# Turning the token rows of a mixture-of-experts stage by DMA instead of TensorE, and putting its last three slot tiles behind a runtime test

## The chip, the cores and the metric

The kernel runs on one core of one Trainium2 chip. The metric is the device time of one execution in microseconds. Three runs of the kernel before gave 461.12, 461.92 and 462.48 us, median 461.92 us. The profile shown below comes from one further execution of 458.04 us, whose span from first to last instruction is 456.3 us.

## The reference

The program is an attention block followed by a top-1 mixture of experts.

```python
q_n, k_n = rmsnorm(q, g_q), rmsnorm(k, g_k)
attn = softmax(q_n @ k_n.T / sqrt(64))          # 8 batches, 12 heads, 448 tokens, 64 wide
x = (attn @ v), heads side by side              # N = 3584 tokens, D = 768
y_dense = relu(x @ w1_dense) @ w2_dense         # hidden width F = 512
e = argmax(x @ w_gate);  g = softmax(x @ w_gate)[e]     # E = 8 experts
y_moe = g * (relu(x @ w1[e]) @ w2[e])
out = y_dense + y_moe
```

The inputs are one fixed draw. On it the eight experts receive 409, 528, 432, 430, 448, 366, 478 and 493 tokens.

## The kernel before

The first part (about 270 us of the span) computes the attention and, for each batch, the gate logits, the chosen expert and the dense hidden layer relu(x @ w1_dense). For each token it writes one record to a DRAM tensor `rec` of 704 words: the token's row x (768 bf16 values), its dense hidden row (512 bf16 values) and its gate weight. This part is the same before and after.

The second part works on *slot tiles*. The tokens of each expert are put into tiles of 128 slots, so that a tile belongs to one expert. The number of tiles depends on the data: it is the sum over the experts of the token count divided by 128, rounded up. The program is written out for the most that can occur, NTL = 28 + 8 - 1 = 35 tiles (`ntl`, `tsi` and `ts` in L536 to L545 count them at run time, and `tsi[E-1]` holds the total). Tiles past the total have no tokens: their scatter is dropped by an out-of-range index (`emp`, L590), but all their work is done.

For each tile t:

- `gather(t)` (L601): POOL issues an indirect DMA that brings 128 records into `xg`, 128 partitions x 704 words.
- `xtrans(t)` (L608): TensorE turns the 6 blocks of x (L612) and the 4 blocks of the dense hidden row (L617), each 128x128 bf16, into two PSUM tiles; VectorE copies them out as `xT` (L614) and `hdT` (L619).
- `gemm1(t)` (L621): TensorE loads the tile's expert number into a register and does 6 matmuls of 512 columns with that expert's w1 (L625); ScalarE applies ReLU and the gate weight, `hs` (L630).
- `htrans(t)` (L632): TensorE turns `hs` in 4 blocks (L635), ScalarE copies them out as `heT` (L637).
- `gemm2(t)` (L639): 8 matmuls with the dense w2 (L644) and 8 with the expert's w2 (L649), 384 columns each, all accumulated into one two-bank PSUM tile `yp`. VectorE copies one half out (L655), ScalarE the other (L656), and POOL issues an indirect DMA that scatters the rows to the output (L657).

The orders of PE and POOL are the order in which the code is written (`manual_schedule(engines={PE, POOL})`). The loop (L673) does for each t: gather(t+4), gemm1(t+1), xtrans(t+2), gemm2(t), htrans(t+1). So one tile's matmuls stand between the steps of its neighbour. The pool that holds the PSUM tile of L656 has one buffer (`psy`, bufs=1).

```python
for t in range(NTL):
    if t + 4 < NTL:
        gather(t + 4)
    if t == 0:
        nc.gpsimd.dma_start(*wjobs[-1])
    if t + 1 < NTL:
        gemm1(t + 1)
    if t + 2 < NTL:
        xtrans(t + 2)
    gemm2(t)
    if t + 1 < NTL:
        htrans(t + 1)
```

Of the kernel before, what the change touches and what calls it, by code (L numbers as in the profile page):

```python
# [9 lines left out]
F32 = mybir.dt.float32  # L10
BF16 = mybir.dt.bfloat16
I32 = mybir.dt.int32
# [6 lines left out]
def kernel(  # L19
# [25 lines left out]
    KD = Dm // P  # L45
    FT = F // P
    HD = Dm // 2
# [10 lines left out]
    ident = const.tile([P, P], BF16)  # L58
# [13 lines left out]
    NTL = N // P + E - 1  # L72
# [3 lines left out]
    GO = XH + F // 2  # L76
    RC = GO + 64
# [56 lines left out]
    with tc.tile_pool(name="a_ld", bufs=2) as ld, \  # L134
# [391 lines left out]
        run({PE, POOL, SP, DVE, ACT})  # L526

    with tc.tile_pool(name="m_sb", bufs=5) as sb, \
         tc.tile_pool(name="m_p1", bufs=3, space=bass.MemoryType.PSUM) as ps1, \
         tc.tile_pool(name="m_p2", bufs=2, space=bass.MemoryType.PSUM) as ps2, \  # L530
         tc.tile_pool(name="m_ph", bufs=1, space=bass.MemoryType.PSUM) as psh, \
         tc.tile_pool(name="m_py", bufs=1, space=bass.MemoryType.PSUM) as psy:

        cnt = counts[B % 2]
        cmp = one.tile([P, E, NM], F32, tag="w1")
# [20 lines left out]
        for c in (slice(0, NC4 // 2), slice(NC4 // 2, NC4)):  # L556
# [3 lines left out]
            for i in range(2):  # L560
                nc.vector.tensor_mul(val[:, i, :, c], tl[:, :, c],
                                     tok[:, i, c].unsqueeze(1).to_broadcast(shape))
        slp = ps2.tile([P, 2, NTL], F32, tag="he")
        for n in range(NC4):
            nc.tensor.matmul(slp, sel[:, n // 4, n % 4], val[:, :, :, n],
                             start=(n == 0), stop=(n == NC4 - 1))
# [10 lines left out]
                                ts[:1].unsqueeze(1).to_broadcast([1, NTL, E]), ALU.is_ge)  # L577
        te = one.tile([1, NTL], F32)
        nc.vector.tensor_reduce(te, tcm, AX.X, ALU.add)
        tei = one.tile([1, NTL], I32)  # L580
        nc.vector.tensor_scalar(tei, te, 1.0, None, op0=ALU.subtract)

# [13 lines left out]
        nc.vector.scalar_tensor_tensor(dest, in0=t2, scalar=float(S - J + 1), in1=emp,  # L596
                                       op0=ALU.subtract, op1=ALU.add)

        xgs, xTs, hdTs, hes, heTs, eregs, stores = {}, {}, {}, {}, {}, {}, []

        def gather(t):  # L601
            xg = sb.tile([P, RC], F32, tag="xg", name="xg")
            nc.gpsimd.indirect_dma_start(  # L603
                out=xg, out_offset=None, in_=rec,
                in_offset=bass.IndirectOffsetOnAxis(ap=row[:, t:t + 1], axis=0))
            xgs[t] = xg

        def xtrans(t):  # L608
            xb = xgs[t].bitcast(BF16)
            xp = ps1.tile([P, KD, P], BF16, tag="tr")  # L610
            for kk in range(KD):
                nc.tensor.transpose(xp[:, kk], xb[:, kk * P:(kk + 1) * P], ident)  # L612
            xTs[t] = sb.tile([P, KD, P], BF16, tag="xT", name="xT")
            nc.vector.tensor_copy(xTs[t], xp)  # L614
            hp = ps1.tile([P, FT, P], BF16, tag="tr")
            for i in range(FT):
                nc.tensor.transpose(hp[:, i], xb[:, Dm + i * P:Dm + (i + 1) * P], ident)  # L617
            hdTs[t] = sb.tile([P, FT, P], BF16, tag="hdT", name="hdT")
            nc.vector.tensor_copy(hdTs[t], hp)  # L619

        def gemm1(t):  # L621
            eregs[t] = nc.tensor.value_load(tei[:, t:t + 1], min_val=0, max_val=min(t, E - 1))
            he = ps2.tile([P, F], F32, tag="he")
            for kk in range(KD):
                nc.tensor.matmul(he, xTs[t][:, kk],  # L625
                                 we[:, bass.ds(eregs[t], 1), 0, kk * F:(kk + 1) * F]
                                 .rearrange("p o f -> p (o f)"),
                                 start=(kk == 0), stop=(kk == KD - 1))
            hes[t] = sb.tile([P, F], BF16, tag="hs", name="hs")
            nc.scalar.activation(hes[t], he, AF.Relu, scale=xgs[t][:, GO:GO + 1])  # L630

        def htrans(t):  # L632
            hp = psh.tile([P, FT, P], BF16, tag="hp")
            for i in range(FT):
                nc.tensor.transpose(hp[:, i], hes[t][:, i * P:(i + 1) * P], ident)  # L635
            heTs[t] = sb.tile([P, FT, P], BF16, tag="heT", name="heT")
            nc.scalar.copy(heTs[t], hp)  # L637

        def gemm2(t):  # L639

            yp = psy.tile([P, 2, 512], F32, tag="y")
            for i in range(FT):
                for dd in range(2):
                    nc.tensor.matmul(yp[:, dd, :HD], hdTs[t][:, i],  # L644
                                     wd2[:, i, dd * HD:(dd + 1) * HD],
                                     start=(i == 0), stop=False)
            for i in range(FT):
                for dd in range(2):
                    nc.tensor.matmul(yp[:, dd, :HD], heTs[t][:, i],  # L649
                                     we[:, bass.ds(eregs[t], 1), 1,  # L650
                                        i * Dm + dd * HD:i * Dm + (dd + 1) * HD]
                                     .rearrange("p o f -> p (o f)"),
                                     start=False, stop=(i == FT - 1))
            ys = sb.tile([P, 2, HD], F32, tag="ys")
            nc.vector.tensor_copy(ys[:, 0], yp[:, 0, :HD])  # L655
            nc.scalar.copy(ys[:, 1], yp[:, 1, :HD])  # L656
            i = nc.gpsimd.indirect_dma_start(  # L657
                out=out, out_offset=bass.IndirectOffsetOnAxis(ap=dest[:, t:t + 1], axis=0),
                in_=ys.rearrange("p a d -> p (a d)"), in_offset=None,
                bounds_check=N - 1, oob_is_err=False)  # L660

            for j in stores:
                tc.declare_no_dep(i.ins, j.ins, reason="each token has one slot")
            stores.append(i)

        with tc.manual_schedule(engines={PE, POOL}):
            for t in range(4):
                gather(t)
            for t in range(2):
                xtrans(t)  # L670
            gemm1(0)
            htrans(0)
            for t in range(NTL):  # L673
                if t + 4 < NTL:
                    gather(t + 4)
                if t == 0:
                    nc.gpsimd.dma_start(*wjobs[-1])
                if t + 1 < NTL:
                    gemm1(t + 1)
                if t + 2 < NTL:  # L680
                    xtrans(t + 2)
                gemm2(t)
                if t + 1 < NTL:
                    htrans(t + 1)


# [28 lines left out]
```

## Time and profile before

| what | value |
|---|---|
| median of 3 runs | 461.92 us |
| profiled execution, its own time | 458.04 us |
| its span | 456.3 us |
| TensorE busy over the span | 384.7 us (84%) |
| VectorE, ScalarE, GpSimd busy | 255.7, 238.8, 240.6 us |
| mean granted TensorE clock | 0.956 of full speed |
| slot tiles: from the first record's arrival to the end | 281.6 to 456.3 us |

The time of an execution is 1.7 us more than its span here, which lies outside the first and last instruction. "Busy" counts an engine's own instructions; TensorE's weight loads run beside its matmuls and are listed as PEld. Issue times of DMAs stand under the queue of the engine that issues them (SPq, POOLq), and the data moves later on 16 shared DMA engines.

### The profile page before, as it was taken

How to read it: one execution, taken by the hardware profiler on the slowest of the kernel's cores; microseconds unless marked ns; L12 is line 12 of the kernel's file. 1: busy time of each engine (PE TensorE's matmuls, PEld its weight loads, DVE VectorE, ACT ScalarE, POOL GpSimd, SP SyncE). 2: the span in 40 equal slices, each digit the busy share in tenths (PEclk: the TensorE clock that was granted, in tenths of full speed). 3: DMA queues.
4: the chain of work that ended last, by engine and by line, in shares of the span. 5: the costliest groups of instructions: out<-in, count | busy, mean ns of one | idle time of the engine just before them, and what ended most of it. 6: DMA issues, size and time to landing. Idle time of an engine off the chain costs nothing.

```text
span 456.3 us, 13950 instructions
## 1 busy us (share of the span) xinstructions
PE 384.7 (84%) x5628; PEld 239.3 (52%) x5628; DVE 255.7 (56%) x744; ACT 238.8 (52%) x394; POOL 240.6 (53%) x275
## 2 busy tenths in 40 slices
PE   0557777988969889798897954899999999999994
PEld 0234554555645556455564633466666666666662
DVE  2565679788897888978875553233232333323230
ACT  2735677785876868768687210333242333334241
POOL 2385887596775877759651105134444353444422
PEclk9999989998998999989999995999999999999998
DMA  8579395977979689796669984553544545354420
GB/s 212 185 112 244 100 249 144 225 153 222 228 229 213 135 241 225 230 213 139 157 100 200 178 194 133 110 172 121 174 129 147 165 137 167 127 171 154 161 95 1
DMA packets 49759, 76.32 MB, mean 167 GB/s; under 512 B 8541, under 2 KB 45661, under 8 KB 49696
## 3 DMA queue, kind: packets, MB, share of 16 engines
q0 software_dynamic: 24544, 43.31, 43.7%
q1 hardware_dynamic: 24832, 32.12, 22.4%
q8 instruction: 46, 0.75, 0.7%
q14 instruction: 17, 0.14, 0.1%
q10 hardware_dynamic: 320, 0.00, 0.0%
HBM read 73.98 MB, written 23.86 MB: 214 GB/s over the span
## 4 chain that ended last, share of the span: by engine, by line
issue 32%; DVE 21%; PE 21%; POOL 16%; ACT 4%; DMA 4%; POOLq 1%; ACTq 0%; DVEq 0%
DVE ssq L192 8%; PE ff L365 8%; POOL xg L603 7%; PE av L259 5%; DVE xa L268 4%; PE sc L241 3%; PE xt L278 3%; POOL out_dram L657 3%; POOL sq L187 3%; DVE y L227 2%; DVE y L229 2%; DMA records<-hd 2%; ACT we L244 2%; DVE y L211 2%; DMA gk<-in_g_k_dram 2%
## 5 line engine op out<-in xcount | busy, mean ns | idle before, releaser
L244 ACT ACTIVATE we<-sc 128x896 bf16<-128x896 f32 x168 | 147.0, 917 | 46.3 <-PE sc L241 45.7
L657 POOL DMA_INDIRECT out_dram<-ys,dest x35 | 35.3, 1010 | 95.2 <-ACT ys L656 90.5
L241 PE MATMUL sc<-y 64*64 64x448 bf16 x672 | 69.9, 408 | 7.9 <-ACT we L244 5.2
L637 ACT COPY heT<-hp 128x512 bf16<-128x512 bf16 x35 | 20.5, 585 | 91.7 <-PE hp L635 91.7
L259 PE MATMUL av<-va,we 64*128 64x65 bf16 x2688 | 63.9, 198 | 4.4 <-issue 3.5
L259 PEld LDWEIGHTS <-we 64*128 64x128 bf16 x2688 | 51.4, 99 | 26.4 <-issue 23.2
L211 POOL TENSOR_TENSOR y<-xk,r 128x448 bf16<-128x448 f32 x46 | 42.1, 937 | 41.7 <-ACT r L205 41.7
L192 DVE TENSOR_REDUCE ssq<-sq 128x7 f32<-128x448 f32 x96 | 55.4, 611 | 12.0 <-POOL sq L187 7.9
L655 DVE COPY ys<-yp 128x384 f32<-128x384 f32 x35 | 19.5, 558 | 72.5 <-issue 55.7
L365 PE MATMUL ff<-wd,xT 128*128 128x512 bf16 x192 | 52.1, 413 | 8.3 <-DVE xa L268 5.6
L625 PE MATMUL he<-we,xT 128*128 (+1 forms) x210 | 52.3, 386 | 0.5 <-issue 0.5
L644 PE MATMUL yp<-wd,hdT 128*128 128x384 bf16 x280 | 51.2, 326 | 1.1 <-ACT ys L656 1.1
L649 PE MATMUL yp<-we,heT 128*128 (+1 forms) x280 | 51.2, 326 | 0.0
L603 POOL DMA_INDIRECT xg<-records,row x35 | 34.5, 986 | 30.4 <-DVE t L591 20.0
L187 POOL TENSOR_TENSOR sq<-xk 128x448 f32<-128x448 f32 x44 | 40.7, 938 | 16.8 <-DVE ssq L192 16.7
L614 DVE COPY xT<-xp 128x768 bf16<-128x768 bf16 x35 | 19.5, 558 | 51.0 <-PE he L625 35.0
L219 PE MATMUL tr<-ident,y 128*128 128x128 bf16 x336 | 26.9, 237 | 20.0 <-DVE y L211 15.0
L268 DVE TENSOR_TENSOR xa<-av,inv 128x256 bf16<-128x256 f32 x96 | 40.8, 425 | 3.3
L187 POOL TENSOR_TENSOR sq<-xq 128x448 f32<-128x448 f32 x44 | 40.1, 932 | 0.0
L630 ACT ACTIVATE hs<-he,xg 128x512 bf16<-128x512 f32 x35 | 24.0, 687 | 27.8 <-PE he L625 18.1
L241 PEld LDWEIGHTS <-y 64*64 64x64 bf16 x672 | 20.5, 107 | 32.9 <-issue 22.9
L649 PEld LDWEIGHTS <-heT 128*128 128x128 bf16 x280 | 27.4, 98 | 18.1
(105 smaller groups left out, 475.6 us busy)
## 6 DMA issues: line engine op xcount, KB each, us to landing
we<-in_moe_w_dram POOLq DMA_DIRECT2D x16, 768.0 KB
xq<-in_q_dram SPq DMA_DIRECT2D x24, 448.0 KB, 4.8
xk<-in_k_dram SPq DMA_DIRECT2D x24, 448.0 KB, 5.7
xv<-in_v_dram POOLq DMA_DIRECT2D x11, 448.0 KB
records<-xa SPq DMA_DIRECT2D x8, 576.0 KB, 9.2
records<-hd SPq DMA_DIRECT2D x24, 128.0 KB, 3.9
wd<-in_moe_w_dense_dram POOLq DMA_DIRECT2D x2, 768.0 KB
records<-xa SPq DMA_DIRECT2D x8, 96.0 KB, 9.0
```

The lines of the kernel that those rows point to most:

```text
L187: nc.gpsimd.tensor_mul(sqs[name, g, hh], x, x)
L192: nc.vector.tensor_reduce(ssqs[g][:, "qk".index(name), hh], sqs[name, g, hh].rearrange("p (j d) -> p j d", d=D), AX.X, ALU.add)
L211: eng.tensor_mul(y[:, :, hh], xin[name, g][:, hh].rearrange("p (j d) -> p j d", d=D), rs[name, g][:, hh].unsqueeze(2).to_broadcast([P, J, D]))
L241: nc.tensor.matmul(ps[r * D:(r + 1) * D, hh, :S], kT[rows, r, j], qT[rows, r].rearrange("p j s -> p (j s)"), start=True, stop=True)
L244: nc.scalar.activation(x, ps[:, :, :S], AF.Exp, scale=scale)
L259: nc.tensor.matmul(avs[hh, r][:, m], exs[g, j][rows, hh, QC[m]:QC[m] + P], va[rows, hh, j, :De], start=(j == 0), stop=(j == J - 1))
L268: nc.vector.tensor_mul(xas[b][:, :, h * D:(h + 1) * D], avs[hh, r][:, :, :D], inv.to_broadcast([P, 4, D]))
L365: nc.tensor.matmul(ff[0], xTs[b][:, kk, QC[m]:QC[m] + P], wd1[:, kk], start=(kk == 0), stop=(kk == KD - 1))
L603: nc.gpsimd.indirect_dma_start(out=xg, out_offset=None, in_=rec, in_offset=bass.IndirectOffsetOnAxis(ap=row[:, t:t + 1], axis=0))
L625: nc.tensor.matmul(he, xTs[t][:, kk], we[:, bass.ds(eregs[t], 1), 0, kk * F:(kk + 1) * F] .rearrange("p o f -> p (o f)"), start=(kk == 0), ...
L644: nc.tensor.matmul(yp[:, dd, :HD], hdTs[t][:, i], wd2[:, i, dd * HD:(dd + 1) * HD], start=(i == 0), stop=False)
L649: nc.tensor.matmul(yp[:, dd, :HD], heTs[t][:, i], we[:, bass.ds(eregs[t], 1), 1, i * Dm + dd * HD:i * Dm + (dd + 1) * HD] .rearrange("p o ...
```

## The change

Only the second part changes.

- The rows of a tile are turned by one DMA transpose from `xg` to `xT`, issued on SP's queue, which carried nothing in this part before. `xT` now holds all 10 blocks, x and dense hidden row. The first two tiles are still turned by TensorE (`turn(t, True)`), now through one PSUM buffer `xp` for both groups of blocks.
- Gathers run five tiles ahead instead of four, with 7 buffers `xg` instead of 5. The transpose of tile t+5 is written right behind its gather.
- `yp` has two PSUM buffers instead of one. The copy of `heT` goes from ScalarE to VectorE.
- The first 32 tiles (NT1 = 28 + 4) are written out as before. All engines then load the run-time total of tiles, `tct`, and the last three tiles stand in a branch that is taken if the total is above 32.

```diff
-         tc.tile_pool(name="m_p1", bufs=3, space=bass.MemoryType.PSUM) as ps1, \
-         tc.tile_pool(name="m_p2", bufs=2, space=bass.MemoryType.PSUM) as ps2, \
-         tc.tile_pool(name="m_ph", bufs=1, space=bass.MemoryType.PSUM) as psh, \
-         tc.tile_pool(name="m_py", bufs=1, space=bass.MemoryType.PSUM) as psy:
+         tc.tile_pool(name="m_ph", bufs=2, space=bass.MemoryType.PSUM) as psh, \
+         tc.tile_pool(name="m_pt", bufs=1, space=bass.MemoryType.PSUM) as pst, \
+         tc.tile_pool(name="m_py", bufs=2, space=bass.MemoryType.PSUM) as psy:
...
+        tct = one.tile([1, 1], I32)
+        nc.vector.tensor_copy(tct, tsi[:1, E - 1:])
...
-            xg = sb.tile([P, RC], F32, tag="xg", name="xg")
+            xg = sb.tile([P, RC], F32, tag="xg", name="xg", bufs=7)
...
-        def xtrans(t):
+        def turn(t, here):
+
+            xTs[t] = sb.tile([P, KD + FT, P], BF16, tag="xT", name="xT")
             xb = xgs[t].bitcast(BF16)
-            xp = ps1.tile([P, KD, P], BF16, tag="tr")
-            for kk in range(KD):
-                nc.tensor.transpose(xp[:, kk], xb[:, kk * P:(kk + 1) * P], ident)
-            xTs[t] = sb.tile([P, KD, P], BF16, tag="xT", name="xT")
-            nc.vector.tensor_copy(xTs[t], xp)
-            hp = ps1.tile([P, FT, P], BF16, tag="tr")
-            for i in range(FT):
-                nc.tensor.transpose(hp[:, i], xb[:, Dm + i * P:Dm + (i + 1) * P], ident)
-            hdTs[t] = sb.tile([P, FT, P], BF16, tag="hdT", name="hdT")
-            nc.vector.tensor_copy(hdTs[t], hp)
+            if not here:
+                nc.sync.dma_start_transpose(xTs[t], xb[:, :2 * GO])
+                return
+            for c in (range(KD), range(KD, KD + FT)):
+                xp = pst.tile([P, KD, P], BF16, tag="xp", name="xp")
+                for i in c:
+                    nc.tensor.transpose(xp[:, i - c[0]], xb[:, i * P:(i + 1) * P], ident)
+                nc.vector.tensor_copy(xTs[t][:, c[0]:c[-1] + 1], xp[:, :len(c)])
...
-            nc.scalar.copy(heTs[t], hp)
+            nc.vector.tensor_copy(heTs[t], hp)
...
-                    nc.tensor.matmul(yp[:, dd, :HD], hdTs[t][:, i],
+                    nc.tensor.matmul(yp[:, dd, :HD], xTs[t][:, KD + i],
...
+        def slots(t0, t1, weights=None):
+            ahead = 5
+            for t in range(t0, min(t0 + ahead, t1)):
                 gather(t)
+            for t in range(t0 + 2, min(t0 + ahead, t1)):
+                turn(t, False)
+            turn(t0, True)
+            gemm1(t0)
+            turn(t0 + 1, True)
+            htrans(t0)
+            for t in range(t0, t1):
+                if t + ahead < t1:
+                    gather(t + ahead)
+                    turn(t + ahead, False)
+                if t == t0 and weights:
+                    nc.gpsimd.dma_start(*weights)
+                if t + 1 < t1:
+                    gemm1(t + 1)
                 gemm2(t)
+                if t + 1 < t1:
                     htrans(t + 1)
...
+        NT1 = N // P + E // 2
+        with tc.manual_schedule(engines={PE, POOL, SP}):
+            slots(0, NT1, wjobs[-1])
+        used = nc.values_load(tct, min_val=1, max_val=NTL)
+        with tc.If(used > NT1):
+            with tc.manual_schedule(engines={PE, POOL, SP}):
+                slots(NT1, NTL)
```

The order of TensorE in one turn of the loop, before, with what each step waits for (the eight rows are where one step ends and the next begins; `xT` and `hdT` are a tile's turned rows, `heT` its turned hidden layer):

```order
L625 LDWEIGHTS xT [waits DVE_49]
...
L612 LDWEIGHTS xg [waits DMASW0_49]
L612 MATMUL xp<-ident,xg 128x128
...
L617 LDWEIGHTS xg
L617 MATMUL hp<-ident,xg 128x128 [waits PE_49]
...
L644 LDWEIGHTS hdT
L644 MATMUL yp<-wd_92,hdT 128x384 [waits Activation_49]
...
L635 LDWEIGHTS hs [waits Activation_49]
```

The same turn after the change:

```order
L626 LDWEIGHTS xT [waits DMAHW3_49]
L626 ISA
L626 MATMUL he<-we,xT 128x512
...
L645 LDWEIGHTS xT
L645 MATMUL yp<-wd_92,xT 128x384
...
L650 LDWEIGHTS heT [waits DVE_49]
...
L636 LDWEIGHTS hs [waits Activation_49]
```

The transposes of L612 and L617 are gone from the turn, the first matmul step waits for a DMA of SP's queue instead of for VectorE, and the dense matmuls no longer wait for ScalarE.

SP's queue from the last store of the first part on, after the change (before, the second row was the last):

```order
L377 DMA records<-hd 128x256 [waits DMAHW2_49,Activation_49]
L377 DMA records<-hd 64x256 [waits DMAHW3_49,Activation_49]
L694 TENSOR_LOAD tct [waits DVE_49]
...
L614 DMA_TRANSPOSE xT<-xg 128x10x128 [waits DMASW3_49]
L614 DMA_TRANSPOSE xT<-xg 128x10x128 [waits DMASW4_49,DVE_49,PE_49]
...
L614 DMA_TRANSPOSE xT<-xg 128x10x128 [waits DMAHW4_49,DMASW1_49,PE_49]
...
L695 COMPARE_AND_BRANCH
```

There are 30 transposes ahead of the branch, one for each of the tiles 2 to 31. Each waits for its gather (a DMASW semaphore) and, through PE, for the matmuls that last read its `xT` buffer, those of the tile five before.

The end of POOL's order after the change:

```order
L658 DMA out_dram<-ys,dest 3584x768 [waits DMASW6_49,Activation_49]
L694 TENSOR_LOAD tct [waits DVE_49]
L695 COMPARE_AND_BRANCH
L604 DMA xg<-records,row 128x704 [waits DMAHW3_49,DMASW7_49]
...
L695 ISA [waits DMASW3_49,DMASW4_49,DMASW2_49,DMASW7_49,DMASW1_49,DMASW0_49]
L695 UNCONDITIONAL_BRANCH
L658 DMA out_dram<-ys,dest 3584x768 [waits DMASW7_49,Activation_49]
```

The first row is the scatter of tile 30, and the last row, which stands behind the branch, that of tile 31: POOL loads the total and branches between the two.

## Rows read from the trace of the kernel before

**Rows 1.** Busy time by stretch: length, engines (instructions), granted clock, DMA share, GB/s.

```profile
270.00:290.00 20.00, 10.84 (x71) 7.34 (x71) 3.91 (x14) 2.36 (x4) 5.78 (x6) 0.66 0.67 168
290.00:340.00 50.00, 50.00 (x391) 31.55 (x389) 15.36 (x32) 17.22 (x31) 20.02 (x20) 1.00 0.42 135
340.00:440.00 100.00, 100.00 (x775) 62.70 (x773) 30.95 (x64) 35.91 (x66) 40.96 (x41) 1.00 0.46 151
```

**Rows 2.** Timeline of one turn: start, length, engine, line, operation, what ended the idle time.

```profile
302.39 0.39 PE L635 MATMUL hp<-ident,hs 128*128 128x128 bf16 x4
...
302.62 1.46 PE L625 MATMUL he<-we,xT 128*128 x6
...
303.91 0.50 PE L612 MATMUL xp<-ident,xg 128*128 128x128 bf16 x6
304.06 1.02 POOL L657 DMA_INDIRECT out_dram<-ys,dest  x1 [2.36 <-ACT ys L656]
...
304.25 0.39 PE L617 MATMUL hp<-ident,xg 128*128 128x128 bf16 x4
...
304.47 1.46 PE L644 MATMUL yp<-wd,hdT 128*128 128x384 bf16 x8
...
305.38 0.99 POOL L603 DMA_INDIRECT xg<-records,row  x1 [0.31 <-issue]
```

**Rows 3.** Timeline: VectorE's copy of `ys` for tile 0, then the last tiles.

```profile
293.24 0.56 DVE L655 COPY ys<-yp 128x384 f32<-128x384 f32 x1 [1.93 <-PE yp L649]
...
442.95 0.56 DVE L655 COPY ys<-yp 128x384 f32<-128x384 f32 x1 [1.99 <-issue]
...
446.81 0.39 PE L635 MATMUL hp<-ident,hs 128*128 128x128 bf16 x4
447.07 0.56 DVE L655 COPY ys<-yp 128x384 f32<-128x384 f32 x1 [3.56 <-PE yp L649]
...
448.31 1.46 PE L644 MATMUL yp<-wd,hdT 128*128 128x384 bf16 x8 [1.11 <-ACT ys L656]
...
449.61 1.46 PE L649 MATMUL yp<-we,heT 128*128 x8
451.16 0.56 DVE L655 COPY ys<-yp 128x384 f32<-128x384 f32 x1 [3.54 <-PE yp L649]
451.75 0.48 ACT L656 COPY ys<-yp 128x384 f32<-128x384 f32 x1 [3.50 <-DVE ys L655]
452.50 0.98 POOL L657 DMA_INDIRECT out_dram<-ys,dest  x1 [2.99 <-ACT ys L656]
```

**Rows 4.** Groups of 290 to 457 us: count, busy us, mean ns of one, idle before.

```profile
L630 ACT ACTIVATE hs<-he,xg 128x512 bf16<-128x512 f32 x34 | 23.4, 687 | 12.2 <-ACT ys L656 9.8 <-PE he L625 2.4
L619 DVE COPY hdT<-hp 128x512 bf16<-128x512 bf16 x33 | 13.7, 415 | 0.0
```

**Rows 5.** DMA queues (packets, MB, share of 16 engines) and loads (KB each, us to landing).

```profile
q0 software_dynamic: 24544, 43.31, 43.7%
q1 hardware_dynamic: 24832, 32.12, 22.4%
q8 instruction: 46, 0.75, 0.7%
...
xk<-in_k_dram SPq DMA_DIRECT2D x24, 448.0 KB, 5.7
```

**Rows 6.** Timeline of the first tiles.

```profile
277.24 1.05 POOL L603 DMA_INDIRECT xg<-records,row  x1 [20.01 <-DVE t L591]
...
281.60 0.80 PE L612 MATMUL xp<-ident,xg 128*128 128x128 bf16 x6 [6.32 <-issue]
...
282.48 0.56 DVE L614 COPY xT<-xp 128x768 bf16<-128x768 bf16 x1 [4.90 <-DMA xg<-records,row]
...
283.55 0.63 PE L617 MATMUL hp<-ident,xg 128*128 128x128 bf16 x4
...
284.01 2.73 PE L625 MATMUL he<-we,xT 128*128 128x512 bf16 x6
...
288.59 1.46 PE L625 MATMUL he<-we,xT 128*128 x6 [0.54 <-issue]
```

More of the change, by code (lines that the diff above doesn't have):

```diff
@@ L562 @@
                                      tok[:, i, c].unsqueeze(1).to_broadcast(shape))
-        slp = ps2.tile([P, 2, NTL], F32, tag="he")
+        slp = psh.tile([P, 2, NTL], F32, tag="he")
         for n in range(NC4):
@@ L597 @@
                                        op0=ALU.subtract, op1=ALU.add)
-        xgs, xTs, hdTs, hes, heTs, eregs, stores = {}, {}, {}, {}, {}, {}, []
+        xgs, xTs, hes, heTs, eregs, stores = {}, {}, {}, {}, {}, []
         def gather(t):
-            xg = sb.tile([P, RC], F32, tag="xg", name="xg")
+            xg = sb.tile([P, RC], F32, tag="xg", name="xg", bufs=7)
             nc.gpsimd.indirect_dma_start(
@@ L606, in gather @@
             xgs[t] = xg
-        def xtrans(t):
+        def turn(t, here):
+            xTs[t] = sb.tile([P, KD + FT, P], BF16, tag="xT", name="xT")
             xb = xgs[t].bitcast(BF16)
-            xp = ps1.tile([P, KD, P], BF16, tag="tr")
-            for kk in range(KD):
-                nc.tensor.transpose(xp[:, kk], xb[:, kk * P:(kk + 1) * P], ident)
-            xTs[t] = sb.tile([P, KD, P], BF16, tag="xT", name="xT")
-            nc.vector.tensor_copy(xTs[t], xp)
-            hp = ps1.tile([P, FT, P], BF16, tag="tr")
-            for i in range(FT):
-                nc.tensor.transpose(hp[:, i], xb[:, Dm + i * P:Dm + (i + 1) * P], ident)
-            hdTs[t] = sb.tile([P, FT, P], BF16, tag="hdT", name="hdT")
-            nc.vector.tensor_copy(hdTs[t], hp)
+            if not here:
[6 more added lines that the diff above has]
+                nc.vector.tensor_copy(xTs[t][:, c[0]:c[-1] + 1], xp[:, :len(c)])
         def gemm1(t):
             eregs[t] = nc.tensor.value_load(tei[:, t:t + 1], min_val=0, max_val=min(t, E - 1))
-            he = ps2.tile([P, F], F32, tag="he")
+            he = psh.tile([P, F], F32, tag="he")
             for kk in range(KD):
@@ L632, in htrans @@
         def htrans(t):
-            hp = psh.tile([P, FT, P], BF16, tag="hp")
+            hp = pst.tile([P, FT, P], BF16, tag="hp")
             for i in range(FT):
@@ L664, in gemm2 @@
             stores.append(i)
-        with tc.manual_schedule(engines={PE, POOL}):
-            for t in range(4):
+        def slots(t0, t1, weights=None):
+            ahead = 5
+            for t in range(t0, min(t0 + ahead, t1)):
                 gather(t)
[L669 to L678, printed above, removed]
+            for t in range(t0 + 2, min(t0 + ahead, t1)):
[11 more added lines that the diff above has]
+                if t + 1 < t1:
                     gemm1(t + 1)
-                if t + 2 < NTL:
-                    xtrans(t + 2)
                 gemm2(t)
-                if t + 1 < NTL:
+                if t + 1 < t1:
                     htrans(t + 1)
+        NT1 = N // P + E // 2
[5 more added lines that the diff above has]
+                slots(NT1, NTL)
 _INS = ['q', 'k', 'v', 'g_q', 'g_k', 'moe_w_gate', 'moe_w1_dense', 'moe_w2_dense', 'moe_w1', 'moe_w2']
```

## The prediction

> **What bounds the kernel now.** I read the busy times by stretch first. From 290 us on TensorE is busy for the whole of every stretch, at the full one of its two clock levels, 2.4 GHz (granted 1.00), while VectorE and ScalarE work for under 40% of the time, POOL for some 40% and the DMA engines for 42% to 46% [rows 1]. So in the slot tiles each microsecond taken from TensorE's own stream is a microsecond of the end, until something else has less slack. The timeline of one turn gives that stream step by step [rows 2]. From the start of one step to the next: htrans 302.39 to 302.62 = 0.23 us, gemm1 302.62 to 303.91 = 1.29, the transposes of x 303.91 to 304.25 = 0.34 and of the hidden row 304.25 to 304.47 = 0.22; the rest are the two halves of gemm2. VectorE's copies of `ys` give the whole turn: from 293.24 (tile 0) to 442.95 (tile 32) are 32 turns, 4.68 us each [rows 3]. The two halves of gemm2 are thus 4.68 - 0.23 - 1.29 - 0.56 = 2.60 us, as the start of the second half, 449.61 - 448.31 = 1.30, confirms [rows 3].
>
> The trace even shows the turn without transposes: tile 33 is the first with none left to do, and its copy comes 447.07 - 442.95 = 4.12 us after the one before [rows 3], which is 4.68 - 0.56.
>
> **The change part by part.** All against the profiled execution: span 456.3 us, time 458.04 us, 3.9 us under the median of 461.92.
>
> *Transposes off TensorE.* The new turn is 4.12 us if the turned row is there in time. *Three tiles less.* The draw gives 4+5+4+4+4+3+4+4 = 32 tiles, so the branch is not taken and tile 31 is the last. Its last turn has no next gemm1: htrans and gemm2, 0.23 + 2.60 = 2.83 us. Before, the copies of tiles 0 and 34 were 451.16 - 293.24 = 157.92 us apart [rows 3]. After, tiles 0 and 31 are 30 x 4.12 + 2.83 = 126.4 us apart. **Gain 31.5 us**, some 17 of it from transposes and 14 from the tiles.
>
> *Second `yp` buffer, `heT` on VectorE.* Nothing on the path. The one wait for `yp` in the rows, 1.11 us for ScalarE's copy, came where a turn had neither gemm1 nor transposes [rows 3]; gemm1 alone (1.29 us) nearly covers it, and the second buffer removes it. VectorE gets a copy of 0.415 us for a tile (the row of the same shape, hdT) and loses 0.97 us; ScalarE keeps 0.687 for `hs` and 0.485 for `ys` [rows 3, 4]. Neither nears 4.12. If that cover were gone, the next to be late would be the copy of `heT`, which has gemm1 and half of gemm2 (2.6 us) to finish.
>
> *Start.* Tiles 0 and 1 stay on TensorE, now through one PSUM buffer: the second group of a tile waits for the copy of the first. Before, gemm1(0) began at 284.01, behind the transposes of both tiles [rows 6]. After: 281.60 + 0.80 + 0.56 (copy) + 0.63 plus two hand-overs of about 0.1 = 283.8; it runs to 286.5 at the low clock level (2.73 us for 6 matmuls that later take 1.29 to the next step) [rows 6]. Tile 1 then takes 0.82 (taken as tile 0's 0.80) + 0.56 + 0.63 + 0.41, so its gemm1 starts near 289.0 against 288.59 [rows 6], but no transposes of tile 2 (0.56) follow. I take 0; between -1 and +2.5, the latter if TensorE, with more gaps here, gets its full clock a few microseconds later (1.2 GHz, half speed).
>
> *Gathers and POOL.* Per turn still one gather (0.99) and one scatter (1.02) [rows 2]. Two more gathers before the loop's first scatter have been issued by 285, ahead of any scatter. Gather t+6 is behind scatter t, about 2.5 us after gemm2(t) ends; it lands some 4.3 us after its issue (277.24 to 281.60) [rows 6], so its transpose can start about 7 us after gemm2(t) and is wanted four turns, 16.5 us, after it. **The transpose has 9 us of latency to spare.** Its `xT` buffer is free earlier, after the first half of gemm2(t+1). Plain loads of 448 KB on SP's queue landed in 5.7 us beside a busier DMA [rows 5]. SP had nothing else to do in this part, so nothing is queued behind its waits but further transposes.
>
> *Transpose rate.* This is the unknown: the trace holds none. One moves 128 x 1,280 bf16 = 327,680 bytes. Today's DMA load per turn is 0.46 of 4.68 us = 2.15 us of all 16 engines for one gather and one scatter, 753,664 bytes [rows 1]. In a turn of 4.12 us it leaves 1.97 us. From below: a transpose priced as these bytes is 327,680/753,664 x 2.15 = 0.93 us, and the engines are 75% busy. From above: SP's shape is 128x10x128, so if each 256-byte row of a block is a packet of its own there are 1,280, and SP's queue has paid 0.224 x 456.3 x 16 / 24,832 = 0.066 us for a packet that was 1.3 KB on average [rows 5]: 1,280 x 0.066 / 16 = 5.3 us. I take under 1.97, because the nearest row is the SP loads, long rows between DRAM and SBUF at 32.12 MB in 22.4% of 16 engines x 456.3 us, 19.6 GB/s an engine, which makes 1.04 us. Then the rate is hidden and costs nothing.
>
> *Branch and end.* The last scatter now stands behind POOL's load of the total and its branch. POOL is free after scatter 30, about 1 us into a last turn of 2.83 us, so some 1.8 us are covered. A branch may have to bring its code: an instruction packet took 0.007 x 456.3 x 16 / 46 = 1.1 us [rows 5]. I take +1 us, between 0 and +4. The Trainium skill (Runtime: NRT & Kernel Launch, Instruction fetch mechanics) speaks against the branch: code is fetched sequentially, and a taken branch outside the two-page window waits for a DMA of the target page. No row here shows one; by that rule this term would stay positive on whichever engine ends last, and 0 would hold only if the target lies in the window.
>
> **Sum:** 458.04 - 31.5 + 0 + 1 = 427.5 us for a profile like this, 461.92 - 30.5 = 431.4, **about 432 us** as a median.
>
> **The rivals.** If transposes come every P us, their stream bounds the end instead: the first starts near 284, the thirtieth lands about 2 us after its slot, and gemm1(31), two gemm2 and htrans (6.7 us) follow it. The copy of tile 31 comes at 292.7 + 30 P, against 293.24 + 126.4 = 419.6 in the forecast. So P counts from 4.23 us on, 30 us for each microsecond, and the gain is used up at P = 4.23 + 30.5/30 = 5.25.
>
> *A. The DMA engines or SP pace the tiles a little.* P between 4.23 and 5.2, for instance a transpose of 2.5 us of all engines: 2.15 + 2.5 = 4.65, and 432 + 30 x 0.42 = 445 us. For it: the engines would be at 100%, and nothing shows a transpose is as cheap as a load. Against: needs twice the price of the nearest row.
>
> *B. Slower: transposes go through the DMA engines as 1,280 short packets.* It decides from P = 5.25, that is from a transpose of 3.1 us. At the upper bound 2.15 + 5.3 = 7.4 us: 432 + 30 x 3.2 = 528 us. TensorE then waits in each gemm1 for SP's DMA. For it: the shape, and that output partitions are written across input rows. Against: the mean price comes from long packets and should overstate short ones. The skill's page Advanced Engine Details and Errata (X-Bar Transpose) says that such DMAs are as fast as regular ones, which would leave 432; the same page (DGE: Hardware vs Software) lists transposes from a hardware queue, such as SP's, as the less efficient kind, without a figure. No run here has shown either.
>
> *C. It doesn't do what it says:* the count exceeds 32 and the branch runs. Three tiles more, 3 x 4.12 us, plus a new start of about 4.3 us (gather) and 7 us (281.60 to 288.59) [rows 6]: 432 + 24 = 456 us. Rounding in bf16 would have to move 16 tokens or more between experts (the nearest limit upwards is expert 5, 366 of 384).
>
> **How the numbers follow.** Forecast 0.66; A 0.15; B 0.17; C 0.02. A measurement of this kernel can tell about 0.3%, 1.4 us. The forecast and C are faster, and of A all but 0.03: faster 0.80, same 0.03, slower 0.17. The forecast's own range is 428 to 436 (start -1 to +2.5, end 0 to +4, partly together). To hold 8 in 10 the range goes on through most of A: 428 to 452; left out are B and the rest of A and C.
>
> **What would show it.** Right: `ys` copies of VectorE every 4.12 us, 32 of them; TensorE busy throughout from 290 us; SP's transposes landing within about 9 us and a DMA share near 0.75; the first matmul of gemm1 not waiting for DMA. A or B: idle time of TensorE in front of gemm1, ended by a DMA that writes `xT`, and copies further apart than 4.12. A wrong end term shows as idle POOL before the last scatter; a wrong start as a first `ys` copy away from 293.2. The prediction is wrong if the transposes' own spacing exceeds 4.23 us.

## The result and the profile after

The changed kernel took 445.43 us (median of 4 runs, 440.51 to 450.19), the kernel before 461.52 us in the same comparison (4 runs, 456.93 to 462.48): a ratio of 0.9635, 95% interval 0.9519 to 0.975. It is faster, as forecast, and inside the stated range of 428 to 452, but 13 us over the predicted 432. The profiled execution took 444.17 us, span 442.5. (Of all profiles below only that of the kernel with the two groups apart is of a disturbed execution, 456.9 us at a lower granted clock; no distance is taken from it.)

Four distances of the two traces tell where the 16.7 us over the predicted span of 425.8 went. The prediction rests on the rows of before in [rows 3, 6].

| distance, us | before | predicted | after |
|---|---|---|---|
| span start to the first gather | 277.24 | 277.24 | 278.86 |
| first gather to the `ys` copy of tile 0 | 16.00 | 16.00 | 16.27 |
| that copy to the copy of the last tile | 157.92 | 126.4 | 137.14 |
| that copy to the end of the span | 5.14 | 6.1 | 10.23 |

The first is the part that the change leaves alone: 1.6 us. Executions with the same code up to there also differ by that much and more (276.7 us with four leading tiles, 282.2 with the late load). The start was as forecast. Missing are 10.7 us in the tiles and 4.1 us at the end.

From the busy times by stretch (length, PE, PEld, DVE, ACT, POOL with counts, clock, DMA share, GB/s) of the kernel after:

```profile
290.00:300.00 10.00, 4.88 (x34) 2.88 (x32) 1.64 (x4) 1.17 (x2) 2.03 (x2) 0.99 1.36 101
300.00:310.00 10.00, 9.76 (x50) 5.17 (x51) 0.89 (x2) 1.85 (x3) 2.01 (x2) 0.83 1.24 144
360.00:380.00 20.00, 19.83 (x128) 11.53 (x126) 3.80 (x9) 5.35 (x9) 9.99 (x10) 1.00 1.10 253
```

Against [rows 1] TensorE lost half of the stretch from 290 us, and the DMA share, 0.46 before, is above 1 through the tiles. Such a share must count packets that are open side by side on one engine, so it is no share of the engines' work. The prediction had 0.75.

The timeline of the first tiles shows the loss:

```profile
278.86 1.05 POOL L604 DMA_INDIRECT xg<-records,row  x1 [18.14 <-DVE t L592]
...
285.99 14.68 SPq L614 DMA_TRANSPOSE xT<-xg  x3
...
286.27 0.84 POOL L682 DMA_DIRECT2D we<-in_moe_w_dram  x1
...
295.13 0.56 DVE L656 COPY ys<-yp 128x384 f32<-128x384 f32 x1 [3.96 <-PE yp L650]
...
300.24 2.58 PE L626 MATMUL he<-we,xT 128*128 x6 [4.92 <-DMA xT<-xg]
302.61 2.07 PE L645 MATMUL yp<-wd,xT 128*128 128x384 bf16 x8
...
306.01 0.56 DVE L656 COPY ys<-yp 128x384 f32<-128x384 f32 x1 [9.99 <-PE yp L650]
```

SP needed 14.68 us to issue three transposes. A weight load of POOL starts 0.3 us behind the first. gemm1 of tile 2 waited 4.92 us for its row. After that idle time TensorE was at the lower of its two clock levels (granted 0.60 from 300 to 302 us and 0.54 from 302 to 304), so gemm1 and half of gemm2 ran some 1.8 us longer. The copies of tiles 0 and 1 are 10.88 us apart instead of 4.12: 6.76 us. Later there are four smaller waits of that kind, 0.56, 0.63, 1.67 and 0.17 us; with their echoes they make the other 4 us. Most turns, 23 of 31, took 4.11 or 4.12 us, as predicted.

The end after the change, by stretch:

```profile
435.00:436.00 1.00, 0.00 (x0) 0.00 (x0) 0.00 (x0) 0.00 (x0) 0.41 (x1) 1.00 0.08 31
436.00:437.00 1.00, 0.00 (x0) 0.00 (x0) 0.00 (x0) 0.00 (x0) 0.00 (x0) 0.97 0.78 310
437.00:438.00 1.00, 0.00 (x0) 0.00 (x0) 0.00 (x0) 0.00 (x0) 0.00 (x0) 0.50 0.00 0
```

And the end of the kernel before:

```profile
454.00:455.00 1.00, 0.00 (x0) 0.00 (x0) 0.00 (x0) 0.00 (x0) 0.00 (x0) 0.50 0.04 1
455.00:456.30 1.30, 0.00 (x0) 0.00 (x0) 0.00 (x0) 0.00 (x0) 0.00 (x0) 0.50 0.02 6
```

Before, the last scatter was that of a tile without tokens: no rows moved (1 and 6 GB/s). Now it is that of tile 31 with 109 rows to store (expert 7 has 493 = 3 x 128 + 109 tokens): 310 GB/s for a microsecond, and then another 5.5 us until the span ends.

### The profile page after: what moved, and what is told of

The parts are those of the page before. It is cut to its first block, busy times and chain, and to the rows that moved or that the text cites. A ratio compares the mean times of both kernels' runs of the same rounds, so it can differ in the third digit from the quotient of the medians.

```text
span 442.5 us, 13009 instructions
## 1 busy us (share of the span) xinstructions
PE 361.0 (82%) x5220; PEld 218.3 (49%) x5220; DVE 235.4 (53%) x708; ACT 218.6 (49%) x353; POOL 234.6 (53%) x269
## 4 chain that ended last, share of the span: by engine, by line
PE 25%; issue 25%; DVE 22%; POOL 15%; DMA 7%; ACT 4%; POOLq 1%; ACTq 0%; DVEq 0%
DVE ssq L192 8%; PE ff L365 8%; POOL xg L604 7%; PE av L259 7%; DMA out_dram<-ys,dest 5%; PE sc L241 5%; DVE xa L268 4%; PE xt L278 3%; POOL sq L187 3%; DVE y L229 2%; DVE y L227 2%; ACT we L244 2%; POOL out_dram L658 2%; DMA gk<-in_g_k_dram 2%; DVE inv L266 1%
## 5 line engine op out<-in xcount | busy, mean ns | idle before, releaser
L658 POOL DMA_INDIRECT out_dram<-ys,dest x32 | 32.3, 1009 | 82.5 <-ACT ys L657 79.8
L259 PE MATMUL av<-va,we 64*128 64x65 bf16 x2688 | 66.4, 201 | 3.6 <-issue 3.2
L259 PEld LDWEIGHTS <-we 64*128 64x128 bf16 x2688 | 53.6, 101 | 26.8 <-issue 23.6
L626 PE MATMUL he<-we,xT 128*128 (+1 forms) x192 | 49.0, 394 | 8.8 <-DMA xT<-xg 8.0
L657 ACT COPY ys<-yp 128x384 f32<-128x384 f32 x32 | 15.3, 479 | 80.6 <-DVE ys L656 75.6
L645 PE MATMUL yp<-wd,xT 128*128 128x384 bf16 x256 | 47.4, 329 | 0.0
L650 PE MATMUL yp<-we,heT 128*128 (+1 forms) x256 | 46.8, 326 | 0.0
L604 POOL DMA_INDIRECT xg<-records,row x32 | 31.5, 985 | 27.6 <-DVE t L592 18.1
L645 PEld LDWEIGHTS <-xT 128*128 128x128 bf16 x256 | 25.3, 99 | 20.4 <-issue 1.1
L219 PEld LDWEIGHTS <-y 128*128 128x128 bf16 x336 | 22.2, 109 | 26.6 <-DVE y L211 15.9
```

Source lines behind the costliest of these rows:

```text
L219: nc.tensor.transpose(ps[:, j], xn[name, g][:, j].rearrange("p h d -> p (h d)"), ident)
L259: nc.tensor.matmul(avs[hh, r][:, m], exs[g, j][rows, hh, QC[m]:QC[m] + P], va[rows, hh, j, :De], start=(j == 0), stop=(j == J - 1))
L604: nc.gpsimd.indirect_dma_start(out=xg, out_offset=None, in_=rec, in_offset=bass.IndirectOffsetOnAxis(ap=row[:, t:t + 1], axis=0))
L626: nc.tensor.matmul(he, xTs[t][:, kk], we[:, bass.ds(eregs[t], 1), 0, kk * F:(kk + 1) * F] .rearrange("p o f -> p (o f)"), start=(kk == 0), ...
L645: nc.tensor.matmul(yp[:, dd, :HD], xTs[t][:, KD + i], wd2[:, i, dd * HD:(dd + 1) * HD], start=(i == 0), stop=False)
L650: nc.tensor.matmul(yp[:, dd, :HD], heTs[t][:, i], we[:, bass.ds(eregs[t], 1), 1, i * Dm + dd * HD:i * Dm + (dd + 1) * HD] .rearrange("p o ...
```

## The experiments

Theories for the stalls: (1) the transposes share the 16 DMA engines with everything else, and these have no slack left at a turn of 4.12 us, so that any burst, the weight load first, stalls TensorE; (2) the transposes or SP's queue are slow by themselves. For the end: (3) the branch or (4) a last scatter that moves rows. "Start", "tiles" and "end" are the last three distances of the table above; "wait" is gemm1's for a transpose.

| kernel | us (median) | start | tiles | end | wait |
|---|---|---|---|---|---|
| the change | 445.43 | 16.27 | 137.14 | 10.23 | 8.0 |
| late load | 448.97 | 16.38 | 139.50 | 10.16 | 11.1 |
| no branch | 442.80 | 16.34 | 139.71 | 9.38 | 10.1 |
| four leading tiles | 439.41 | 22.91 | 127.96 | 10.16 | 1.4 |
| branch alone | 451.17 | 17.29 | 143.89 | 9.40 | none |
| early load | 438.28 | 15.80 | 133.04 | 10.16 | 5.0 |
| before, 32 tiles | 445.93 (one run) | 16.22 | 143.89 | 9.36 | none |
| every fourth on TensorE | 445.25 | 16.20 | 135.99 | 10.15 | none |
| every eighth on TensorE | 443.47 | 15.94 | 131.89 | 10.13 | none |

The waits are those that the trace puts down to the transpose's DMA. The medians are of runs on several chips; the kernel before had between 458.95 and 465.48 us beside them, so the distances within a profile tell more than the medians.

**Late load.**

```diff
-                if t == t0 and weights:
+                if t == t0 + 2 and weights:
```

> The change with the last weight load (768 KB, second matrix of expert 7) issued two turns later. Theory one (the load holds up the first transposes on the DMA engines): the transposes of tiles 2 to 4, which took 14.7 us of SP's queue, take 6 us or less, gemm1 of tile 2 no longer waits, the gap between the first two copies of ys falls from 10.88 to about 4.1 us, and the time is 6 to 8 us under the change's. Theory two (three transposes in a row are slow by themselves): the gap stays over 8 us and the time within 2 us of the change's. If the load only moves the collision, the gap moves to turns 3 to 6.

The first gaps became 4.12 us each, and gaps of 14.11 and 7.19 us came at the sixth and seventh. TensorE's timeline with the load on POOL:

```profile
306.31 0.86 POOL L682 DMA_DIRECT2D we<-in_moe_w_dram  x1
```

```profile
318.93 0.39 PE L636 MATMUL hp<-ident,hs 128*128 128x128 bf16 x4
327.34 2.72 PE L626 MATMUL he<-we,xT 128*128 x6 [8.02 <-DMA xg<-records,row]
...
336.56 1.24 PE L626 MATMUL he<-we,xT 128*128 x5 [3.13 <-DMA xT<-xg]
```

The stall went where the load went, as the last sentence of what was expected has it, though a little later; so the time did not fall, 448.97 us. The first of these waits is put down to a gather, but the weight load in front of the same matmul waited as long for the transpose:

```profile
PEld L626 <- DMA xT<-xg: 11.1, 2, 8.1
```

That transpose, tile 7's, was issued at 310.63 us, 4.3 us behind the load, and the matmul that needed it began at 327.34.

**Early load.** The load joins the three that end the first part.

```diff
-                while nw[0] < len(wjobs) - 1:
+                while nw[0] < len(wjobs):
...
-            slots(0, NT1, wjobs[-1])
+            slots(0, NT1)
```

> The change with the last weight load issued ahead of the gathers, with the three weight loads that end the first part, where the change's DMA engines were 42% busy between 270 and 280 us. Theory one (that load is what the first transposes wait behind): no wait of gemm1 for a transpose at the start, first gap between copies of ys 4.12 us, the distance from first to last copy 126.4 to 129 us against 137.1, and the time 6 to 8 us under the change's, if the first gather's rows land no more than 1 us later. Rival one: the load holds up the gathers instead, the first record arrives 3 to 6 us later after its issue (4.4 us in the change), and the time stays within 2 us of the change's. Rival two (transposes in a row are slow by themselves): the gap stays above 8 us.

The stall at the start is gone (first gap 4.12 us), the first record came 3.9 us after its issue, and the time was 438.28 us (434.10 to 443.83; ratio to before 0.9474, 0.9259 to 0.9689, which overlaps the change's). So the load was what the first transposes stood behind. The distance is not 126.4 to 129 but 133.04 us: three stalls remain in the middle of the stage, where no load runs:

```profile
359.23 1.24 PE L626 MATMUL he<-we,xT 128*128 x5 [0.45 <-DMA xT<-xg]
365.75 2.72 PE L626 MATMUL he<-we,xT 128*128 x6 [2.46 <-DMA xT<-xg]
398.32 1.24 PE L626 MATMUL he<-we,xT 128*128 x5 [2.10 <-DMA xT<-xg]
```

The trace shows where the second of them begins:

```profile
348.97 0.98 POOL L604 DMA_INDIRECT xg<-records,row  x1 [0.30 <-issue]
```

This is the gather of tile 19. SP had nothing to issue from 350.57 us until the row had landed, at 358.76, 9.8 us after the gather's issue; then came the transpose, and the matmul began at 365.75. The two took 16.8 us, where the loop had left 14.3 (2.46 less). So no transposes had queued up on SP: the gather was late, not only the transpose. In the kernel of the change, too, SP mostly waits for gathers (total us, times, longest):

```profile
SPq L614 <- DMA xg<-records,row: 74.2, 24, 8.9
```

Theory one covers this if the engines' load is what delays the gather. A third theory fits as well: a lead of five tiles is too short for a gather and a transpose that land one after the other. No kernel with a longer lead and nothing else changed was run.

**Four leading tiles on TensorE.** The load stays in its place; tiles 2 and 3 are turned ahead of the loop.

```diff
-            for t in range(t0 + 2, min(t0 + ahead, t1)):
+            for t in range(t0 + 4, min(t0 + ahead, t1)):
                 turn(t, False)
...
             htrans(t0)
+            for t in range(t0 + 2, min(t0 + 4, t1)):
+                turn(t, True)
```

> The change with four leading tiles turned by TensorE instead of two. The 768 KB load stays where it is. Both theories of the start expect gemm1 of tile 2 not to wait. Theory one (the load in the way): the transpose of tile 4 is wanted two turns later, near 304 us, and is in time, so the time falls by 4 to 6 us (the stall, less 1.1 us of TensorE). Rival (transposes run too slowly at the start whatever their number): the stall moves to gemm1 of tile 4 or 5 and the time falls by under 2 us.

No wait at the start, one of 1.4 us later, and 127.96 us between the copies, the least of any complete kernel. But the start grew from 16.3 to 22.9 us:

```profile
288.71 0.49 PE L619 MATMUL xp<-ident,xg 128*128 128x128 bf16 x6 [0.29 <-DVE xT L620]
...
291.90 0.59 PE L619 MATMUL xp<-ident,xg 128*128 128x128 bf16 x4 [0.65 <-DVE xT L620]
...
292.81 2.72 PE L626 MATMUL he<-we,xT 128*128 x6 [0.32 <-issue]
295.32 2.76 PE L645 MATMUL yp<-wd,xT 128*128 128x384 bf16 x8
```

Two tiles more through one PSUM buffer took 4 us, not 1.1, with TensorE waiting for VectorE's copies, and at the end of it the granted clock was the lower level again (0.50 from 292 to 298 us; 2.72 and 2.76 us for steps of 1.3). The median of 439.41 us is about that of the early load.

**Every transpose twice.** This prices one.

```diff
                 nc.sync.dma_start_transpose(xTs[t], xb[:, :2 * GO])
+                spare = sb.tile([P, KD + FT, P], BF16, tag="spare", name="spare", bufs=2)
+                nc.sync.dma_start_transpose(spare, xb[:, :2 * GO])
```

> The change with every DMA transpose issued twice, the second time into a tile that nobody reads. This prices one transpose. If it costs 2.6 us of all 16 DMA engines (what the change's queue share gives), the turn is set by the DMA engines at 2.15 + 5.2 = 7.3 us and the time is 85 to 100 us over the change's. If it costs only 1.0 us (the price that the prediction took), 2.15 + 2.0 = 4.2 us, and the time rises by under 10 us.

501.59 us, 56 over the change: between the two. The copies of tiles 0 and 31 (297.33 and 489.69) are 192.4 us apart, a mean turn of (192.4 - 2.83)/30 = 6.32 us. (The 5.95 in the next expectation is too low.) If the DMA engines set it, 6.32 = 2.15 + 2 x 2.08: by this estimate a transpose takes 2.08 us of all engines, and one in each turn needs 2.15 + 2.08 = 4.23 us, just over the 4.12 that TensorE needs. The next kernel makes it a range, 1.7 to 2.2 us. TensorE's waits in that kernel and the queue of its DMAs:

```profile
PE he L628 <- DMA xT<-xg: 51.5, 15, 9.8
```

```profile
q1 hardware_dynamic: 103552, 51.79, 48.9%
```

Against [rows 5] there are 103,552 - 24,832 = 78,720 packets more for 60 transposes, 1,312 for each, some 250 bytes long.

**Twice, with few scatters.** Is it the engines, or SP's queue?

```diff
+            if t % 8:
+                return
             i = nc.gpsimd.indirect_dma_start(
                 out=out,
```

> Every DMA transpose issued twice, and the scatter of the output left out for seven tiles of eight (their rows are computed and copied, not stored). With all scatters the mean turn was 5.95 us. Theory one (the 16 DMA engines set the pace: 2.15 us for gather and scatter and 1.9 us for each transpose): the scatter is 52% of 2.15 us by its bytes, seven eighths of it are 0.98 us, so the mean turn falls to about 5.0 us. Theory two (SP's queue sets the pace with some 2.9 us for each transpose, whatever else the engines move): it stays at 5.7 to 5.95 us.

The distance is 162.28 us, a mean turn of 5.32 us: 1.00 us less than with all scatters, where seven eighths of a scatter were priced at 0.98. That the two agree is luck: the first two gaps, in the stall at the start, took 29.84 us here and 8.24 with all scatters. The 28 turns behind them took 4.63 us in the mean, against 6.47: 1.84 us less. SP's issue of the second transpose fell from 3.26 to 1.63 us in the median. A queue with a fixed pace would not have gained. Theory two falls, more clearly than by the expected number.

But one price does not give both. With 2.15 us for the rest, 6.47 makes a transpose 2.16 us; with 2.15 - 0.98 = 1.17, 4.63 makes it 1.73, and that at most, since most of these turns took TensorE's own 4.12. So I take **1.7 to 2.2 us** of all engines, an estimate; one in each turn then needs 3.9 to 4.3 us, on both sides of 4.12. That the engines are overloaded in the steady loop is not shown.

**Once, early load, few scatters.** The edits of the early load and of the kernel before this one, with single transposes.

> The kernel with the early weight load, every transpose once, and the scatter left out for seven tiles of eight. With all scatters the copies of ys of tiles 0 and 31 were 133.0 us apart, 6.6 us of it in stalls of gemm1 for a transpose in the middle of the stage. Theory one (the DMA engines are 98% loaded at a turn of 4.12 us and have no slack for a disturbance): with about 3.1 us of load per turn no such stall is left, 126.4 to 127 us. Theory two (stalls come from the transposes or SP alone): stalls of several us remain.

No gemm1 waited for a transpose, and the DMA share fell below 1 through most of the tiles:

```profile
300.00:340.00 40.00, 39.13 (x245) 22.66 (x249) 8.66 (x20) 10.45 (x19) 11.44 (x12) 1.00 0.83 160
340.00:380.00 40.00, 39.14 (x241) 22.38 (x244) 7.92 (x19) 10.33 (x18) 11.55 (x13) 1.00 0.85 175
```

The distance, 129.27 us, is above the expected 127: three times VectorE's copy of a `ys` came some 2 us late and `heT` behind it. These are not the stalls in question. Each of the three copies begins 9.0 us after a scatter's issue began (302.65 and 311.67 us for the first), but nothing in the trace names the scatter as what held it, and the cause stays open. The kernel also does not part theory one from the third: without most scatters POOL issues gathers earlier, five between 303.99 and 309.96 us, so both the load and the lead changed.

**Every fourth and every eighth tile on TensorE.** With the early load and a sixth `xT` buffer (shown for every eighth; the other has 4 and 1 for 8 and 5).

```diff
...
-                    turn(t + ahead, False)
+                    if (t + ahead) % 8 != 5:
+                        turn(t + ahead, False)
...
                     gemm1(t + 1)
+                if t + 2 < t1 and t + 2 >= t0 + ahead and (t + 2) % 8 == 5:
+                    turn(t + 2, True)
                 gemm2(t)
```

> The kernel with the early weight load, and every fourth tile from tile 5 on (7 tiles) turned by TensorE again. TensorE's own stream grows by 7 x 0.56 = 3.9 us. DMA load falls to 2.15 + 0.75 x 1.9 = 3.6 us of a mean turn of 4.26. Theory one: no stalls are left, the copies of tiles 0 and 31 are 130.3 to 132 us apart, and the time is 1 to 4 us under that of the early load alone (438.3) and steadier. Theory two: stalls as before, time 2 to 5 us over it.

> The same with every eighth tile (tiles 5, 13, 21 and 29). TensorE gets 4 x 0.56 = 2.2 us more, DMA load 2.15 + 0.875 x 1.9 = 3.8 us of 4.19. Theory one: stalls become rare, 128.7 to 131 us between the copies of tiles 0 and 31, time 2 to 4 us under that of the early load alone. Theory two: stalls as before.

In both profiles no gemm1 waits for a transpose; the DMA share from 300 to 420 us is 0.85 and 0.89. That an eighth less is always enough is not shown: the next kernel, with the same tiles on TensorE, has one such wait of 7.17 us. And a tile on TensorE costs 5.48 - 4.12 = 1.36 us, not 0.56, so the distances are 126.4 + 7 x 1.36 = 135.9 and 126.4 + 4 x 1.36 = 131.8, as measured. TensorE in such a turn:

```profile
301.73 0.50 PE L619 MATMUL xp<-ident,xg 128*128 128x128 bf16 x6
302.88 0.38 PE L619 MATMUL xp<-ident,xg 128*128 128x128 bf16 x4 [0.65 <-DVE xT L620]
303.10 1.46 PE L645 MATMUL yp<-wd,xT 128*128 128x384 bf16 x8
```

The second group waits for the copy of the first out of the one buffer. So every fourth tile gains nothing, 445.25 us. Every eighth is not told apart from the early load: 443.47 us in the median, but two of its four runs, 436.08 and 439.64 us, lie among the early load's 434.10 to 443.83.

**The two groups apart.** Blocks of x ahead of gemm2, blocks of the hidden row behind it.

```diff
...
+                here = t0 + ahead <= t + 2 < t1 and (t + 2) % 8 == 5
+                if here:
+                    turn(t + 2, True, (0,))
                 gemm2(t)
+                if here:
+                    turn(t + 2, True, (1,))
```

> Early weight load, and tiles 5, 13, 21 and 29 turned by TensorE, with the six blocks of x ahead of gemm2 and the four blocks of the hidden row behind it, so that the second group no longer waits for the copy of the first. In the kernel that did both groups at once such a turn took 5.48 us, 1.36 over the plain 4.12. Theory (0.80 us of that is the wait for the single PSUM buffer): such a turn takes 4.12 + 0.56 = 4.68 us, the copies of tiles 0 and 31 are 126.4 + 4 x 0.56 = 128.7 us apart (131.9 in that kernel, 133.0 with the early load alone), no gemm1 waits for a transpose by more than 1 us, and the profiled time is near 433 us. Rival: the copy of the hidden blocks now comes late for the dense matmuls, and the turn stays above 5.2 us.

440.38 us (7 runs, 438.86 to 456.9; ratio 0.9586, 0.9527 to 0.9646), no gain over the early load that the runs could show. The shape of such a turn:

```profile
309.02 0.50 PE L620 MATMUL xp<-ident,xg 128*128 128x128 bf16 x6
309.36 1.46 PE L646 MATMUL yp<-wd,xT 128*128 128x384 bf16 x8
310.66 1.46 PE L651 MATMUL yp<-we,heT 128*128 x8
313.24 0.40 PE L620 MATMUL xp<-ident,xg 128*128 128x128 bf16 x4 [1.12 <-DVE xT L621]
```

Although a whole gemm2 lies between the groups, the second still waits 1.12 us for VectorE's copy of the first, which in VectorE's own order comes late: at 312.63 us, behind the `ys` copy of 312.16, for blocks that TensorE had turned by 309.52. The expectation of 4.68 us fails. So does that of no wait above 1 us, at least in this execution (the one of 456.9 us):

```profile
419.09 2.72 PE L627 MATMUL he<-we,xT 128*128 x6 [7.17 <-DMA xT<-xg]
```

**No branch.** Last four rows of the change taken out; the last three tiles, empty on this draw, are left out.

```diff
-        used = nc.values_load(tct, min_val=1, max_val=NTL)
-        with tc.If(used > NT1):
-            with tc.manual_schedule(engines={PE, POOL, SP}):
-                slots(NT1, NTL)
```

> The change without the load of the total and without the branch: 32 tiles are written out and the last three are left out of the program (on this draw they are empty). Theory: the branch is what makes the span end 10.2 us after the last copy of ys starts, where it was 5.1 us before. Then that distance is 5 to 7 us here and the time 4 to 5 us under the change's. Rival: the distance is that of a last scatter that moves data (the scatter that ended the kernel before moved none); then it stays near 9 to 10 us and the time within 1.5 us of the change's.

The end is 9.38 us: the rival is right, though the time, 2.6 us under the change's, missed its 1.5. The load of the total and the branch cost 10.2 - 9.4 = 0.8 us, ahead of the last scatter: after ScalarE's last copy the scatter starts 435.86 - (435.11 + 0.48) = 0.27 us later here, 434.42 - (432.86 + 0.48) = 1.08 us later in the change. The chain that ended last runs over POOL's own instructions of the branch line there, up to 433.54 us; the scatter's row puts its wait down to ScalarE's queue at the same line. I take POOL, but the two are not told apart. The stall at the start was 8.76 us in this execution, against 4.92 with the same code up to there: its size varies.

**The branch alone, and 32 tiles of the kernel before.** The kernel before with the run-time total and the branch:

```diff
...
+        NT1 = N // P + E // 2
+        with tc.manual_schedule(engines={PE, POOL}):
+            slots(0, NT1, wjobs[-1])
+        used = nc.values_load(tct, min_val=1, max_val=NTL)
+        with tc.If(used > NT1):
+            with tc.manual_schedule(engines={PE, POOL}):
+                slots(NT1, NTL)
```

> The kernel before, with its transposes on TensorE, and of the change only the run-time total and the branch over the last three tiles. The turn stays 4.68 us, tile 31 is the last. Less by three tiles: 157.92 - (30 x 4.68 + 4.12 - 1.29) = 14.7 us. If the end costs 5 us as in the change, the time is 9 to 10 us under the kernel before (ratio 0.979); if the end costs nothing by itself, 14 to 15 us (ratio 0.968).

And with the loop and its bounds cut to 32:

```diff
+        NU = 32
...
-            for t in range(NTL):
+            for t in range(NU):
...
```

> The kernel before with its loop cut to 32 tiles, without any branch; the three tiles without tokens are left out. Theory of the end (a last scatter that moves rows ends later than one whose rows are all dropped): the span ends 8.5 to 9.4 us after the last copy of ys starts, against 5.14 us. Rival (the branch makes the end long): 5.1 to 5.5 us. Either way the distance from first to last copy is 143.9 us, as with the branch alone.

Both have 143.89 us between the copies and ends of 9.40 and 9.36 us. Without any branch the end is 4.2 us longer than the 5.14 of the kernel before, because its last scatter stores rows; with the branch it costs nothing more, since the last turn there is 4.09 us long and hides POOL's part (its instructions of the branch end at 437.7 us, ScalarE's last copy at 438.67). With the branch alone the ratio is 0.9787 (0.9593 to 0.9982). So of the change's gain of 16 us about 10 are the three tiles. The rest I put down to the transposes; the second `yp` buffer and the copy of `heT` on VectorE were not tried by themselves.

## Why the prediction came out as it did

- *The bound and the turn: right.* TensorE set the pace, and 4.12 us, read from one turn of the trace before, is the turn of most tiles.
- *Three tiles less: right in the stream, wrong at the end.* 14 us were gained in the tiles and 4.2 given back. The step "Branch and end" took the end of the kernel before as it was and added 1 us for the branch. That end belonged to a scatter of dropped rows, although the text itself says that tiles past the total move nothing. The branch was priced well, 0.8 us for 1, but by a packet of code, which no run shows: POOL's compare and branch took 0.05 us, its load of the total 0.51, and the longest piece is a semaphore instruction of the branch line, 1.70 us, ending at 433.54. The Trainium skill's rule (Runtime: NRT & Kernel Launch, Instruction fetch mechanics), that a branch out of the window waits for its code, has the sign of that term; whether any of the 0.8 us is such a wait was not measured.
- *Start: right* in its sum (16.27 against 16.00). *Rival C* did not come; its 16 tokens should have been 19 (385 - 366).
- *"The transpose has 9 us of latency to spare": failed at tile 2.* The step counted the transposes of the steady loop and took 5.7 us for a landing. It did not count the weight load that the loop issues next to the first ones, though the order of POOL shows it there. Cost: 6.8 us in the profile. The late and the early load show the cause. In the middle of the stage the same step was too generous: it took 4.3 us for a gather's landing beside the transposes, too, and measured were 5.7 in the median and up to 13.4 (300 to 432 us), with 5.6 for a transpose behind it. Some 4 us went there; whether to full engines or to too short a lead stays open.
- *Transpose rate, "I take under 1.97": mis-sized.* The doubled transposes give 1.7 to 2.2 us, about twice the 0.93 by bytes and the 1.04 of the row taken as nearest, well under the upper bound of 5.3. So by this estimate the engines are not 75% busy but near their limit. Rival B had the packets right (1,312 against 1,280) and their price wrong: 21 to 27 ns (1.7 to 2.2 us x 16 / 1,312), not 66. At 3.9 to 4.3 us the need lies about the 4.23 from which the text lets P count, and the loop nearly keeps pace, with little reserve. The Trainium skill (Advanced Engine Details and Errata, X-Bar Transpose) has transposes as fast as regular DMAs; by the 0.93 us that the same bytes take in gather and scatter they run at about half of that here, and the measurement decides.
- *The range* held, because rival A was in it. Its signs came: TensorE idle in front of gemm1 for a DMA that writes `xT`, and SP's transposes 4.56 us apart in the mean, (418.1 - 286.0) / 29, beyond the 4.23 that the text names as refuting its forecast. Its price, 445 us, was met by luck: by a burst at the start, scattered stalls and the end, not by one slow pace. Of the 30 us forecast as gain 16 came.

## What to carry to other kernels

Moving work from the busiest engine to the DMA engines is only free while their load per turn, old and new together, stays clearly under the turn; near equality a burst such as the weight load becomes a stall, so look for the bursts (a late weight load) and move them out first. Count latency by the landing times under the new load, not those of the old trace. When the last pieces of a loop go, the end of the program is no longer that of the old trace: ask what the new last instruction moves. A spare buffer given away (one PSUM tile instead of three for a transpose) costs more than the transposes themselves once TensorE has to do them again, 0.80 us a tile against 0.56 here.

## What the runs showed of the hardware

SP's issue of one 128 x 1,280 transpose took 1.25 us at the least, 1.73 in the median and 9.24 beside the weight load, and with every transpose doubled the second one's issue fell from 3.26 to 1.63 us in the median when most scatters went: the time of the issue depends on what else the engines move. A last scatter of 109 rows keeps the span open for 9.4 us after the last copy begins, one whose rows are all dropped for 5.1, none at all for 2.3 (the kernel with few scatters, span 432.9, last copy 430.56).
